# First block sums of a two-level Strassen output: a unit later by DMA in three units of four, on VectorE in the fourth

## The chip, the cores and the metric

One NeuronCore of a Trainium2 chip runs the whole program. The metric is the device time of one execution in microseconds (us). Engine names: PE is TensorE, PEld its weight loads, DVE VectorE, ACT ScalarE, POOL GpSimd, SP SyncE; the q after a name (SPq, POOLq) marks the engine's own queue.

## The reference

The program computes a channel attention and then a SiLU feed-forward network on its output:

```python
qn = q / (norm(q, axis=1) + 1e-6);  kn = k / (norm(k, axis=1) + 1e-6)   # q, k, v: (2, 6016, 256)
s = kn.transpose(0, 2, 1) @ qn / tau                                    # (2, 256, 256)
a = softmax(s)
x = (v @ a).reshape(12032, 256)
h = x @ w_in                                                            # w_in: (256, 2048)
out = (h / (1 + exp(-h))) @ w_out                                       # w_out: (2048, 256)
```

All in float32. On the chip, every operand of a large product is kept as two float16 parts (high and low), and a product is three float16 matmuls.

## The kernel before

The 12032 tokens are cut into 12 "pairs" `p` of two token blocks, 1024 tokens wide (896 in pairs 5 and 11). Pairs 0 and 5 run an older path (`emit_pair_group`, L682, 8 groups each; "the old pairs"), the other ten the path with units (`emit_unit`, L729, 8 units `u` each, 80 in all; `paired` holds these pairs). In the paired pairs the order of PE, DVE and ACT is the order in which the code writes the instructions; POOL and SP are ordered by a scheduler.

A unit works on one half of the pair's tokens (`t = u // 4`) and a quarter of the hidden width (`q = u % 4`), in four slots, one after each `yield`. Its seven input products go into three PSUM banks `y`, `x`, `z`, allocated once at L48. Slot 0 writes y, x and z; slot 1 adds to y and x; slot 2 and slot 3 add to x. ACT copies y and x out (L780, L782, L790), DVE takes differences (L760), ACT applies SiLU (L763) and makes the high parts of the hidden blocks (L770), DVE the low parts (L773). Four blocks come out of a unit: b11, b12 (the "tops") and b21, b22 (the "lows").

`out_of_unit` (L852 to L971) is the output side. Per unit it queues eleven "items" of four matmuls each on average (`add`, line L866 of the trace) into the list `ready`. They accumulate in four PSUM banks per half, a, b, c and d, from a pool of four (`ps_o`). Some items read the blocks, four read sums of blocks: t1 = b11 + b12, t3 = b12 + b22, t2 = t3 + b11, t4 = t2 + b21. The sums t2 and t3 are two DVE instructions in slot 2 of the next unit (`plus`, L940). The sum t1 is made by POOL's DMA queue in `first_sum`: a copy of b11 into a buffer (L946), then, when it has landed, an accumulating copy of b12 on top (L949). The sum t4 is made in the same way a unit later (copy of t2, L948; accumulating copy of b21, L951), except in the last unit of a half (`own`), where DVE makes it. In the trace L946 and L949 are t1's two DMAs, L948 and L951 are t4's, and the matmuls of t1 read `sums` with the weights `ws_lo`/`ws_hi`, those of t4 read `sums` with `wo`.

The code of unit u's output side runs as a list of steps by slot (`later`): in unit u+1, slot 0 the low part of the tops, `first_sum` and the high part of the lows; in slot 1 the low part of the lows; in slot 2 `other_sums`, which appends the unit's items to `ready`. After each slot the main loop runs items from `ready`: 2, 3, 4 and 2 of them in slots 0 to 3 (`room_left` 8, 12, 16, 8 at cost 4). So the eleven items of unit u run from slot 2 of unit u+1 to slot 1 of unit u+2, and the last of them reads t1. t4's item of unit u is put just ahead of t1's item of unit u+1 (`behind_one`).

After the last unit of a half (q = 3) the four banks are copied out by ACT (`take`, L910): c, a, b, d in slots 0, 1, 2, 3 of unit u+2. In slot 3 DVE also combines them (`join`, four L925 instructions, and `leave(0)`, one L929 and a store); `leave(1)` (L929, store) is in slot 0 of unit u+3.

In the same slots DVE and ACT prepare the next pair's operand (`scale_v`, 15 steps). They are taken in units 2, 3, 4, 6 and 7, in three slots each: slots 1 to 3 up to pair 3, slots 0 to 2 from pair 4 on. The load of the next v (`load_v`, L485, 1 MB on SP) starts when the buffer of the last one is free.

Of the kernel before, what the change touches and what calls it, by code (L numbers as in the profile page):

```python
# [8 lines left out]
F16 = mybir.dt.float16  # L9
# [9 lines left out]
P = 128  # L19
# [11 lines left out]
def channel_attention_then_silu_ffn(ctx, tc, kq, qT, kT, vT, tau, w_in, w_out, outT):  # L31
# [13 lines left out]
    hp = ctx.enter_context(tc.tile_pool(name="hp", bufs=1))  # L45
    sm = ctx.enter_context(tc.tile_pool(name="sm", bufs=2))
    ps_b = ctx.enter_context(tc.tile_pool(name="ps_b", bufs=1, space=PSUM))
    z, y, x = (ps_b.tile([P, 512], F32, tag=k, name=k) for k in "zyx")  # L48
    ps_o = ctx.enter_context(tc.tile_pool(name="ps_o", bufs=4, space=PSUM))

    ident = const.tile([P, P], F32, name="ident")
# [13 lines left out]
    rtau = const.tile([P, 1], F32, name="rtau")  # L65
    tiny = const.tile([P, 1], F32, name="tiny")
    nc.vector.memset(tiny, 1e-30)
    junk = const.tile([1, 1], F32, name="junk")
    ws_hi = const.tile([P, 4, NI, P], F16, name="ws_hi")

# [20 lines left out]
    def small_psum(name):  # L91

        if early[0]:
            return ps_o.tile([P, 512], F32, tag="o", name=name)
        return z

    @contextmanager
    def at(priority):
# [583 lines left out]
    def emit_pair_group(p, i):  # L682
# [7 lines left out]
        def product(bank, a, x, first=False):  # L690
            for j, (u, y) in enumerate(((1, 0), (0, 1), (0, 0))):
                nc.tensor.matmul(
                    bank[:, :h], wm[:, u, a - 1], m[:, y, x, :h], start=(first and j == 0),
                    stop=(j == 2), skip_group_check=True,
                )

        def copy(bank, t):
            nc.scalar.copy(t[:, :h], bank[:, :h])
            return t
# [8 lines left out]
        def silu(src, g, row, l):  # L708
            nc.scalar.activation(out=g[:, :h], in_=src[:, :h], func=AF.Silu, scale=alpha)
            return {"p": p, "f": 2 * i + (row == 1), "l": l, "h": h, "g": g, "sg": sg}  # L710

        product(y, S1, T1, True)
        c51 = hp.tile([P, 2, 512], F32, tag="c51", name="c51")
        c5 = copy(y, c51[:, 0])
        product(x, A11, B11, True)
        c1 = copy(x, c51[:, 1])
        product(z, A12, B21, True)
        g11 = minus(c1, z)
        tail(0)
# [20 lines left out]
    def emit_unit(p, u):  # L740
# [2 lines left out]
        b, n, w = pairs[p]  # L743
        h = w // 2
        m, alpha, sg = parts[p]
        which = 2 * (u % 4), 2 * (u % 4) + 1
        wide = h // 2
        at = u // 4 * wide
# [80 lines left out]
    def out_of_unit(p, u, blocks, rest_top, high_low, rest_low):  # L829
# [10 lines left out]
        if "14" not in sums:  # L840
            sums["14"] = vp.tile([P, 2, 2, 2, 512], F16, tag="v", name="sums", bufs=3)
        t23 = st.tile([P, 2, 2, 512], F16, tag="st", name="t23", bufs=7)
        w1, w4 = (sums["14"][:, u % 2, k] for k in range(2))
        t1, t4, t2, t3 = (k[:, :, :h] for k in (w1, w4, t23[:, 0], t23[:, 1]))

        def bank(name):
# [28 lines left out]
        def cross(kind, e, x):  # L875
            return [(kind, e, x, 1, 0), (kind, e, x, 0, 1)]

        def high(e, x1, x2):
# [8 lines left out]
            add("d", 0, high(1, b11, b21), False),  # L887
            add("d", 1, high(1, b12, b22), end),
        ]
        fourth = add("d", 0, cross(0, 1, t4), end)  # L890
        then = [
            add("a", 1, cross(-2, 1, t2), end),
            add("b", 0, cross(-3, 1, t3), end),
            *behind_one,
            add("b", 1, cross(-1, 1, t1), end),
        ]
        behind_one[:] = []
        if own:
            then.append(fourth)
        else:  # L900
            behind_one.append(fourth)
        s = {}

        def take(name):
# [34 lines left out]
        def plus(o, x, y):  # L939
            nc.vector.tensor_tensor(out=o, in0=x, in1=y, op=ALU.add)  # L940

        def first_sum():
            if last:
                plus(t1, b11, b12)
                return
            nc.gpsimd.dma_start(w1, blocks[0])  # L946
            for o, x, y in fourths:
                nc.gpsimd.dma_start(o, x)  # L948
            nc.gpsimd.dma_start(w1, blocks[1], accum_op=ALU.add)  # L949
            for o, x, y in fourths:  # L950
                nc.gpsimd.dma_start(o, y, accum_op=ALU.add)  # L951
            fourths[:] = []

        def other_sums():
            ready.extend(now)
            plus(t3, b12, b22)
            plus(t2, t3, b11)
            if own:
                plus(t4, t2, b21)
            else:  # L960
                fourths.append((t4, t2, b21))
            ready.extend(then)
# [2 lines left out]
        later(1, rest_low)  # L965
        later(2, other_sums)
        if end:
            for k, name in enumerate("cabd"):
                later(4 + k, lambda name=name: take(name), order=1)
            later(7, join, lambda: leave(0), order=2)  # L970
            later(8, lambda: leave(1), order=2)  # L971

    def prepare_sums():

# [274 lines left out]
    fixed = ExitStack()  # L1249
    for p, (b, n, w) in enumerate(pairs):  # L1250
        fixed.close()
        if p in paired:
            fixed.enter_context(
                tc.manual_schedule(
                    engines={
                        mybir.EngineType.PE, mybir.EngineType.DVE, mybir.EngineType.Activation
                    }
                )
            )
# [5 lines left out]
        for i in range(NI):  # L1265
# [30 lines left out]
            for _ in (emit_unit if p in paired else emit_pair_group)(p, i):  # L1296
# [3 lines left out]
                if p == 0 and i < 2:  # L1300
                    prepare()
                take = 2 if p == 0 and i > 2 and len(pending) > 4 - slot else 1
                room_left = (8, 12, 16, 8)[slot] if p in paired else 12 * take
                queue = ready if p in paired else pending
                while queue and room_left > 0:
                    cost, run = queue.pop(0)
# [3 lines left out]
                if p == 0 and i < NI - 1:  # L1310
                    nextmix = background(nextmix)
                if p in paired:
                    if i in (2, 3, 4, 6, 7) and slot in ((1, 2, 3) if p < 4 else (0, 1, 2)):
                        vgen = background(vgen)
                elif i >= 1 and vgen is not None and (
                    p == 0 or slot in ((0, 2) if not last else (0, 2, 3) if i > 4 else (2, 3))
                ):
                    vgen = background(vgen, 2 if p == 0 else 1)
# [62 lines left out]
```

## Time and profile before

| what | us |
|---|---|
| median of 3 runs (lowest to highest) | 1063.17 (1061.96 to 1067.81) |
| the profiled execution, its own time | 1060.87 |
| its span in the trace | 1059.1 |
| PE busy | 1015.2 (96%) |
| DVE busy | 831.7 (79%) |
| ACT busy | 800.8 (76%) |
| POOL busy | 207.7 (20%) |
| mean granted TensorE clock | 0.989 |

The span is what the trace shows from the first to the last event; the execution's own time is 1.8 us more. A busy share is a mean over the whole span; PE's includes time at either clock level.

### The profile page before, as it was taken

How to read it: one execution, taken by the hardware profiler on the slowest of the kernel's cores; microseconds unless marked ns; L12 is line 12 of the kernel's file. 1: busy time of each engine (PE TensorE's matmuls, PEld its weight loads, DVE VectorE, ACT ScalarE, POOL GpSimd, SP SyncE). 2: the span in 40 equal slices, each digit the busy share in tenths (PEclk: the TensorE clock that was granted, in tenths of full speed). 3: DMA queues.
4: the chain of work that ended last, by engine and by line, in shares of the span. 5: the costliest groups of instructions: out<-in, count | busy, mean ns of one | idle time of the engine just before them, and what ended most of it. 6: DMA issues, size and time to landing. Idle time of an engine off the chain costs nothing. (4 is left out here: it accounts for less than half of the span.)

```text
span 1059.1 us, 20486 instructions
## 1 busy us (share of the span) xinstructions
PE 1015.2 (96%) x8222; PEld 841.5 (79%) x8222; DVE 831.7 (79%) x1339; ACT 800.8 (76%) x1161; POOL 207.7 (20%) x299
## 2 busy tenths in 40 slices
PE   9999999998999799999999999999999999999985
PEld 8876555787888688878655688888888888889985
DVE  6998577778779588978789788888788878888764
ACT  6687687887778579778778778778678787787763
POOL 0010000122221222222100022222222222222231
PEclk9999999999999899999999999999999999999998
DMA  9996010557546465544301244545545445444442
GB/s 369 395 400 207 1 40 1 173 134 219 162 120 165 138 189 138 142 103 100 101 20 32 65 114 111 146 109 135 135 97 155 118 98 148 120 104 120 112 113 65
DMA packets 62544, 143.34 MB, mean 135 GB/s; under 512 B 6898, under 2 KB 19010, under 8 KB 62450
## 3 DMA queue, kind: packets, MB, share of 16 engines
q0 software_dynamic: 31696, 72.57, 29.4%
q1 hardware_dynamic: 30466, 68.95, 18.5%
q8 instruction: 64, 1.05, 0.4%
q10 hardware_dynamic: 288, 0.52, 0.1%
q14 instruction: 30, 0.25, 0.1%
HBM read 57.67 MB, written 12.32 MB: 66 GB/s over the span
## 5 line engine op out<-in xcount | busy, mean ns | idle before, releaser
L753 PEld LDWEIGHTS <-wall 128*128 128x128 f16 x3360 | 328.4, 98 | 49.4 <-issue 12.9
L753 PE MATMUL x<-m,wall 128*128 128x256 f16 (+1 forms) x1920 | 260.7, 272 | 8.4 <-ACT c L790 3.5
L773 DVE SCALAR_TENSOR_TENSOR hl<-g,sg,hl 128x1024 f16<-128x1024 f32 (+1 forms) x160 | 203.0, 1269 | 76.1 <-ACT hl L770 74.8
L866 PE MATMUL o<-hl,wo 128*128 128x256 f16 (+1 forms) x1920 | 248.7, 273 | 0.5 <-DVE hl L773 0.5
L866 PEld LDWEIGHTS <-wo 128*128 128x128 f16 x2240 | 220.3, 99 | 27.9 <-issue 2.9
L763 ACT ACTIVATE g<-g,alpha 128x1024 f32<-128x1024 f32 (+3 forms) x160 | 146.0, 927 | 88.7 <-DVE g L760 86.5
L770 ACT ACTIVATE hl<-g,sg 128x1024 f16<-128x1024 f32 (+1 forms) x160 | 181.5, 1135 | 0.0
L753 PE MATMUL y<-m,wall 128*128 128x256 f16 (+1 forms) x960 | 129.8, 271 | 0.1
L949 POOL DMA_DIRECT2D sums<-hl x79 | 67.2, 851 | 278.7 <-DMA sums<-hl 206.6
L946 POOL DMA_DIRECT2D sums<-hl x79 | 57.9, 733 | 227.7 <-DMA outT<-sb 103.8
L951 POOL DMA_DIRECT2D sums<-hl x59 | 51.8, 878 | 184.9 <-DMA sums<-t 48.4
L760 DVE TENSOR_TENSOR g<-x,c 128x512 f32<-128x512 f32 (+1 forms) x80 | 54.5, 681 | 42.6 <-PE x L753 42.5
L661 PE MATMUL o<-hl,wo 128*128 128x512 f16 (+1 forms) x384 | 87.2, 366 | 0.1
L790 ACT COPY c<-x 128x512 f32<-128x512 f32 (+1 forms) x80 | 46.5, 581 | 54.0 <-PE x L753 53.8
L866 PEld LDWEIGHTS <-ws_hi 128*128 128x128 f16 x640 | 62.9, 98 | 29.8 <-issue 23.0
L763 ACT ACTIVATE g<-x,alpha 128x512 f32<-128x512 f32 (+1 forms) x80 | 54.3, 679 | 29.9 <-PE x L753 27.7
L866 PE MATMUL o<-t,ws_lo 128*128 128x256 f16 (+1 forms) x320 | 76.7, 271 | 0.0
L866 PE MATMUL o<-t,ws_hi 128*128 128x256 f16 (+1 forms) x320 | 76.7, 271 | 0.0
L760 DVE TENSOR_TENSOR g<-c,y 128x512 f32<-128x512 f32 (+1 forms) x80 | 54.3, 679 | 28.3 <-ACT c L790 27.8
L300 PE MATMUL sc<-kq_t 128*128 128x256 f32 x320 | 74.6, 385 | 0.5 <-DMA kq_t<-in_kq 0.4
L300 PEld LDWEIGHTS sc<-kq_t 128*128 128x128 f32 x320 | 61.0, 193 | 11.6 <-DMA kq_t<-in_kq 1.7
L661 PEld LDWEIGHTS <-wo 128*128 128x128 f16 x384 | 37.6, 98 | 39.1 <-issue 0.9
(194 smaller groups left out, 1608.0 us busy)
## 6 DMA issues: line engine op xcount, KB each, us to landing
sums<-hl POOLq DMA_DIRECT2D x212, 256.0 KB, 3.3
kq_t<-in_kq SPq DMA_DIRECT2D x39, 512.0 KB, 8.8
sums<-t POOLq DMA_DIRECT2D x54, 256.0 KB, 2.8
v_t<-in_vT SPq DMA_DIRECT2D x10, 1024.0 KB, 6.2
outT<-sb SPq DMA_DIRECT2D x40, 256.0 KB, 2.5
turned<-in_qT SPq DMA_DIRECT2D x10, 512.0 KB, 4.8
turned<-in_kT SPq DMA_DIRECT2D x10, 512.0 KB, 5.7
raw<-in_w_in SPq DMA_DIRECT2D x5, 512.0 KB, 10.5
```

Source lines behind the costliest of these rows:

```text
L300: nc.tensor.matmul(sc[:, cb, :], t[:, i, 0, cb * P : (cb + 1) * P], t[:, i, 1, :], start=(j + i == 0 and cb == 0), stop=(j + i == J - 1), ...
L661: nc.tensor.matmul(o[:, :h], a[:, f, ee], hl[:, m, :h], start=(c == 1 and i == 0), stop=(c == NF and i == 2),)
L753: nc.tensor.matmul(bank[:, k * wide : (k + 1) * wide], mixed[b, i][:, v, a - 1], m[:, c, x, at : at + wide], start=(first and j + k == 0), ...
L760: nc.vector.tensor_tensor(out=g, in0=a[:, :h], in1=c[:, :h], op=ALU.subtract)
L763: nc.scalar.activation(out=g, in_=src, func=AF.Silu, scale=alpha)
L770: nc.scalar.activation(out=hl[:, :, 0], in_=g, func=AF.Copy, scale=sg)
L773: nc.vector.scalar_tensor_tensor(out=hl[:, :, 1], in0=g, scalar=sg, in1=hl[:, :, 0], op0=ALU.mult, op1=ALU.subtract,)
L790: nc.scalar.copy(c2[:, :h], x[:, :h])
L866: nc.tensor.matmul(o[:, side * wide : (side + 1) * wide], a, x, start=(first and j == 0), stop=(last and j == len(these) - 1), skip_group_ ...
L946: nc.gpsimd.dma_start(w1, blocks[0])
L949: nc.gpsimd.dma_start(w1, blocks[1], accum_op=ALU.add)
L951: nc.gpsimd.dma_start(o, y, accum_op=ALU.add)
```

## The change

- t1 of a unit that is not `own` is still made by DMA, but its item (with t4's item) moves to the end of the next unit's list: `others` in `behind_one`. It needs one more buffer, `extra`.
- In an `own` unit (the fourth of each half; in the last half also the third) DVE makes t1, as one more `plus` in `other_sums`, into a tile of its own with t4 (`t14`, from the pool of `st` buffers). `first_sum` then issues only t4's DMAs of the unit before.
- The copies out of the banks: c, a as before, b one slot later (slot 3 of unit u+2), d one slot later (slot 0 of unit u+3), `leave(0)` in slot 0 and `leave(1)` in slot 1 of unit u+3.
- The 15 steps of `scale_v` are spread 3, 4, 1, 3, 4 over units 2, 3, 4, 6, 7 instead of 3 each.
- In the last unit of the program 3 items instead of 4 run in slot 2, and none in slot 3 (`over`); the rest follows after it.
- y, x and z are allocated per group in the old pairs, and once per run of paired pairs in the others (`firsts`).

```diff
-    z, y, x = (ps_b.tile([P, 512], F32, tag=k, name=k) for k in "zyx")
+    firsts = {}
+    extra = const.tile([P, 2, 512], F16, name="extra")
-        return z
+        return firsts["z"] if firsts else ps_b.tile([P, 512], F32, tag="z", name=name)
 # emit_pair_group
+        y = ps_b.tile([P, 512], F32, tag="y", name="y")
+        x = ps_b.tile([P, 512], F32, tag="x", name="x")
...
+        z = ps_b.tile([P, 512], F32, tag="z", name="z")
 # emit_unit
+        if not firsts:
+            firsts.update({k: ps_b.tile([P, 512], F32, tag=k, name=k) for k in "zyx"})
+        x, y, z = (firsts[k] for k in "xyz")
 # out_of_unit
-        w1, w4 = (sums["14"][:, u % 2, k] for k in range(2))
+        w1, w4 = (*(sums["14"][:, k, 0] for k in range(2)), extra)[q % 3], sums["14"][:, q % 2, 1]
+        if own:
+            t14 = st.tile([P, 2, 2, 512], F16, tag="st", name="t14", bufs=7)
+            w1, w4 = (t14[:, k] for k in range(2))
-        fourth = add("d", 0, cross(0, 1, t4), end)
+        others = [add("b", 1, cross(-1, 1, t1), end), add("d", 0, cross(0, 1, t4), end)]
             *behind_one,
-            add("b", 1, cross(-1, 1, t1), end),
+            *(others if own else ()),
         ]
-        behind_one[:] = []
-        if own:
-            then.append(fourth)
-        else:
-            behind_one.append(fourth)
+        behind_one[:] = [] if own else others
         def first_sum():
-            if last:
-                plus(t1, b11, b12)
-                return
-            nc.gpsimd.dma_start(w1, blocks[0])
-            for o, x, y in fourths:
+            these = [*([] if own else [(w1, *blocks[:2])]), *fourths]
+            for o, x, y in these:
                 nc.gpsimd.dma_start(o, x)
-            nc.gpsimd.dma_start(w1, blocks[1], accum_op=ALU.add)
-            for o, x, y in fourths:
+            for o, x, y in these:
                 nc.gpsimd.dma_start(o, y, accum_op=ALU.add)
 # other_sums
             if own:
+                plus(t1, b11, b12)
                 plus(t4, t2, b21)
         if end:
-            for k, name in enumerate("cabd"):
-                later(4 + k, lambda name=name: take(name), order=1)
-            later(7, join, lambda: leave(0), order=2)
-            later(8, lambda: leave(1), order=2)
+            for k, name in (4, "c"), (5, "a"), (7, "b"), (8, "d"):
+                later(k, lambda name=name: take(name), order=1)
+            later(7, join, order=2)
+            later(8, lambda: leave(0), order=2)
+            later(9, lambda: leave(1), order=2)
 # main loop
+        if p not in paired:
+            firsts.clear()
-                room_left = (8, 12, 16, 8)[slot] if p in paired else 12 * take
+                over = p == len(pairs) - 1 and i == NI - 1
+                room_left = (8, 12, 16 - 4 * over, 8 - 8 * over)[slot] if p in paired else 12 * take
-                    if i in (2, 3, 4, 6, 7) and slot in ((1, 2, 3) if p < 4 else (0, 1, 2)):
+                    many = {2: 3, 3: 4, 4: 1, 6: 3, 7: 4}.get(i, 0)
+                    if slot in ((), (3,), (), (1, 2, 3) if p < 4 else (0, 1, 2), range(4))[many]:
                         vgen = background(vgen)
```

## Rows read from the trace of the kernel before

**Rows 1.** The page: busy time, share and instructions of each engine.
```profile
PE 1015.2 (96%) x8222; PEld 841.5 (79%) x8222; DVE 831.7 (79%) x1339; ACT 800.8 (76%) x1161; POOL 207.7 (20%) x299
```
**Rows 2.** PE's longest wait over the span: us in total, times, longest.
```profile
PE o L866 <- DMA sums<-hl: 22.9, 10, 4.4
```
**Rows 3.** PE's groups by shape: count, busy, mean ns, idle before them and what ended it.
```profile
L866 PE MATMUL o<-sums,ws_lo 128*128 128x256 f16 x144 | 35.9, 276 | 13.1 <-DMA sums<-hl 12.9
...
L866 PE MATMUL o<-sums,ws_lo 128*128 128x224 f16 x16 | 3.9, 272 | 8.0 <-DMA sums<-hl 8.0
```
**Rows 4.** Stretches at half clock: length, then busy PE, PEld, DVE, ACT, POOL, PEclk, DMA.
```profile
263.98:267.38 3.40, 2.92 (x14) 2.02 (x14) 0.60 (x1) 0.00 (x0) 0.97 (x2) 0.50 0.20 82
345.90:356.13 10.23, 5.85 (x29) 4.19 (x28) 2.67 (x4) 0.72 (x1) 3.05 (x5) 0.50 0.59 162
1045.63:1049.03 3.40, 2.70 (x15) 2.20 (x15) 0.56 (x1) 0.00 (x0) 0.00 (x0) 0.50 0.05 8
```
**Rows 5.** Timeline at one wait: start, length, engine, line; in brackets the idle time before.
```profile
253.81 0.38 SPq L485 DMA_DIRECT2D v_t<-in_vT  x1
254.28 1.86 SPq L256 DMA_DIRECT2D turned<-in_qT  x3
...
256.10 0.85 POOL L949 DMA_DIRECT2D sums<-hl  x1 [3.29 <-DMA sums<-hl]
...
264.45 0.37 PE L866 MATMUL o<-sums,ws_lo 128*128 128x256 f16 x1 [3.35 <-DMA sums<-hl]
```
**Rows 6.** Timeline of POOL and PE in an undisturbed unit.
```profile
860.93 0.86 POOL L946 DMA_DIRECT2D sums<-hl  x1
...
866.57 0.85 POOL L949 DMA_DIRECT2D sums<-hl  x1 [4.78 <-DMA sums<-hl]
...
870.27 0.60 PE L866 MATMUL o<-sums,wo 128*128 128x256 f16 x4
...
870.70 0.27 PE L866 MATMUL o<-sums,ws_lo 128*128 128x256 f16 x1
```
**Rows 7.** DMAs into `sums`: us from issue to landing, least, median, most.
```profile
DMA to landing us min/median/max: 2.3/3.3/9.5
```
**Rows 8.** Timeline at the one wait of t4's item.
```profile
345.31 0.60 PE L866 MATMUL o<-sums,wo 128*128 128x256 f16 x4 [1.92 <-DMA sums<-hl]
```
**Rows 9.** Timeline of PE and ACT in slot 0 of a unit with a copy out.
```profile
867.65 0.60 PE L866 MATMUL o<-hl,wo 128*128 128x256 f16 x4
868.73 0.68 ACT L910 ACTIVATE sb<-o,back 128x512 f32<-128x512 f32 x1
```
**Rows 10.** Timeline of DVE and PE in unit 2 of a pair from pair 6 on.
```profile
838.15 1.28 DVE L773 SCALAR_TENSOR_TENSOR hl<-g,sg,hl 128x1024 f16<-128x1024 f32 x1
...
839.35 0.68 DVE L929 TENSOR_TENSOR sb<-sb 128x512 f32<-128x512 f32 x1
...
839.95 0.68 DVE L760 TENSOR_TENSOR g<-c,z 128x512 f32<-128x512 f32 x1
...
845.32 0.82 PE L753 MATMUL x<-m,wall 128*128 128x256 f16 x6 [0.38 <-DVE g L760]
```
**Rows 11.** Timeline of DVE and PE in unit 6 of a pair from pair 6 on.
```profile
882.36 0.68 DVE L760 TENSOR_TENSOR g<-x,c 128x512 f32<-128x512 f32 x1
...
883.09 0.81 PE L753 MATMUL x<-m,wall 128*128 128x256 f16 x6
```
**Rows 12.** DVE's block sums by shape, and DVE's wait for the lows' and tops' high parts.
```profile
L940 DVE TENSOR_TENSOR t<-hl 128x1024 f16<-128x1024 f16 x72 | 49.1, 682 | 0.0
...
DVE hl L773 <- ACT hl L770: 74.8, 82, 3.2
```
**Rows 13.** PE's wait in slot 2 after a copy out and a square on ACT (pair 1).
```profile
233.14 0.81 PE L753 MATMUL x<-m,wall 128*128 128x256 f16 x6 [0.19 <-ACT c L790]
```
**Rows 14.** Timeline of the end: DVE's last low part and PE's last wait for a sum.
```profile
1043.01 1.15 DVE L773 SCALAR_TENSOR_TENSOR hl<-g,sg,hl 128x896 f16<-128x896 f32 x1
...
1046.33 0.35 PE L866 MATMUL o<-sums,ws_lo 128*128 128x224 f16 x1 [4.38 <-DMA sums<-hl]
```

## The prediction

> **What bounds the kernel now.** I read the page first: PE is busy in 96% of the span, DVE and POOL far less [rows 1], so time can only be won where PE stands still or runs slowly, and it is lost where another engine makes PE wait. The view of PE's waits then names one cause that is larger than all others together: the output products wait for DMAs into `sums`, 22.9 us in 10 waits [rows 2]. The groups by shape say which product that is: t1's items, with 12.9 us in the wide pairs and 8.0 us in the narrow last one [rows 3]; what is left, 1.9 us, is a single wait of t4's item [rows 8].
>
> The timeline shows why. In an undisturbed unit t1's copy is issued at 860.93 and the accumulating copy at 866.57, because POOL waits for the landing in between; with the median landing of 3.3 us [rows 7] the sum is there at 869.9, and its item starts at 870.70 [rows 6]: 0.8 us to spare. Where a load of v and three more loads are issued just ahead (253.81 and 254.28), the accumulating copy of 256.10 is late: the item starts at 264.45, 8.35 us after its issue, having waited 3.35 us [rows 5]. So t1 is nearly late in every unit, and any load on the DMA queues turns that into a wait of PE.
>
> Three of these waits also cost clock. In the stretches at half clock (0.50 is the lower of the two levels, 1.2 GHz) PE worked for 2.92, 5.85 and 2.70 us [rows 4]. Each begins while PE stands still for a sum. Half of that work, 11.47 / 2 = 5.7 us, would be saved at full clock. The waits and the clock together are 28.6 us.
>
> The Trainium skill ("TensorE: Matmul & The Clock Gate", Terms) puts the penalty at the time below full rate times the share of pulses lost; that is 17.03 x 0.5 = 8.5 us by the lengths of the same stretches. The rows decide here: in 5.6 us of these stretches PE had nothing to do, and that time is already in the waits.
>
> **t1 a unit later (three units of four).** Nothing changes in the work of PE: the same four matmuls run, ten items on average further down. A unit is 9.4 us long (x in slot 3 of two units that lie four apart starts at 845.32 and 883.09, [rows 10, 11]; the difference over 4). t1's room grows from 0.8 to about 10 us, and the longest landing in the whole trace, 9.5 us against a median of 3.3 [rows 7], is only 6.2 us over. I take all of t1's waits, 20.9 us, as gone in these units.
>
> **t1 on DVE (one unit of four).** Twenty more sums of 0.68 us [rows 12], 13.6 us of DVE, one in each unit after an `own` unit; the one of the last unit was there already, and the third unit of the last half adds one more. They stand in slot 2 behind PE's needs of that slot. DVE afterwards waits for ACT's high part in most units, 74.8 us in 82 waits, 0.9 us each [rows 12], which is more than 0.68. Units 4 and 0 have the added sum; unit 4 gives up two preparation steps and unit 0 has none. I take 0. If that cover were gone it would cost 20 x 0.68 = 13.6 us at most. POOL loses 40 DMAs, and so 40 x 256 KB of traffic; I count nothing for it.
>
> **t4 stays where it was.** Its DMAs are issued in the same slot as before and its item moves back by one item, 0.43 us (four matmuls; 870.70 - 870.27 in [rows 6]). The one wait of 1.92 us [rows 8] then leaves 1.5 us. Beside it, the fourth sum of the next unit queues on POOL behind the late t1 and may be late once or twice: I take 2.0 us in all, bounds 0 and 8 (four such waits of 2).
>
> **The copies out.** c and a keep their slots. b goes into slot 3, d into slot 0 of the next unit, behind the high part of the lows. On ACT this moves 0.68 us into slot 0. Behind it there stand the copy of c2 (L790), for which PE's x product of slot 2 waits, and in pairs 1 to 3 a square of 1.05 us. The same sequence stands in the trace already, one unit earlier, with the copy of c: there PE's x product waited 0.19 us [rows 13]. Six such halves (pairs 1 to 3) give 1.1 us; bounds 0 and 4 (six times 0.7).
>
> On DVE `leave(0)` comes into slot 0 where `leave(1)` was, and `leave(1)` into slot 1, ahead of the two differences on which x in slot 3 waits. In unit 2 from pair 4 on, where two maxima of v are in the way, PE already waits 0.38 us for DVE there. One more L929 takes 0.60 us of a busy DVE (839.35 to 839.95); `leave(0)` used to stand ahead of 838.15 and gave 0.15 of that [rows 10], so PE's wait grows by 0.45. In unit 6 the difference ends at 883.04 and x starts at 883.09 [rows 11]: no cover is left, so 0.45 to 0.5 us there as well. Six pairs (4, 6 to 10) times two halves times 0.47 are 5.7 us. In pairs 1 to 3 slot 0 has no preparation step in these units, which leaves some 0.7 us or more of cover: nothing. Bounds: 0 and 12 (1 us in each of the 12).
>
> **The rest.** In the last unit x of slot 3 runs one item earlier (0.4 us), and PE has those items left while ACT and DVE finish the last blocks. Its wait of 4.38 us for t1 goes. What is late next is DVE's last low part, which ends at 1044.16 [rows 14], some 0.4 us earlier after the change; the items that PE still has reach to about 1043. I take 0.5 us of wait, bounds 0 and 1.5. In the old pairs PE is without gaps before, so new tiles of x, y and z can win nothing there; a worse order may cost up to 3 us, and I take 0. A PE that is not held up meets ACT and DVE less rested: 1 us, bounds 0 and 3, for the short waits that the stalls now hide.
>
> **The sum.** -28.6 + 2.0 + 1.1 + 5.7 + 0.5 + 1.0 = -18.3 us against the profiled execution's own 1060.87 us (span 1059.1 and 1.8 around it): 1042.6. The median of the runs is 2.3 us above that execution; such a spread is what late DMAs make, and most of them go, so I forecast 1043. With all costs at their low ends (0) it is 1060.87 - 28.6 = 1032; with t4, DVE and ACT at their high ends (8, 12 and 4) and 2 for the rest it is 1058.
>
> **Rivals.** (1) The wait moves from t1 to t4. POOL takes its DMAs in a scheduled order, and up to now t4's go ahead of t1's. If t1's went first, t4 would inherit the 0.8 us to spare. Each of nine waits would then be shorter only by the item's 0.43 us, about 4 us in all, with one of three clock losses gone, 2 us; with the costs above the time would be 1060.9 - 6 + 7 = 1062, no change. Against it: t4's inputs are ready a slot or more ahead of t1's, and in the trace its item waits once in the whole span. The Trainium skill ("DMA: Bandwidth & Descriptors", Anatomy of one DMA) puts a GpSimd DMA at 2.0 us plus its bytes over 436 GB/s, by my estimate 2.6 us for 256 KB. By that no sum would ever be late and this rival, like the gain, would be nothing; the 8.35 us of [rows 5] says otherwise, so the rows decide.
>
> (2) Slower: PE waits for the copy out of d. The next half's first product into its bank d is the second item of slot 0 of unit u+3, the very slot into which d's copy moves. PE reaches the second item 0.43 us after 867.65, at 868.08; a copy out in that place starts at 868.73 and ends at 869.41 [rows 9]: 1.3 us of wait. This happens in 18 changes of half: 18 x 1.3 = 24 us, and with the sum above 1067. It decides if the new d is given the bank of the old d. The pool hands out the bank that came free first, and that is b's, copied out a slot earlier; new b then takes d's. The order of copies out and of first products speaks for this, no row shows the bank.
>
> (3) DVE becomes the bound in units 6 and 7, and 2 and 3. It has four steps in units 3 and 7 now, behind units 2 and 6 with two `leave`s. If each of 20 halves costs 0.8 us instead of 12 costing 0.47, that is 16 us instead of 5.7: 1053.
>
> (4) The change does not do what it says: the loads that made t1 late make something else late (the loads wait for `st` buffers, of which `t14` takes one), and the time stays near 1060.
>
> **Chances.** The forecast 0.66 (1035 to 1050 by its own range), rival 1 0.07, rival 2 0.10, rival 3 0.12, rival 4 0.05. What a measurement of this kernel can tell from no change is about 0.5%, 5.3 us, so faster means under 1057.9 and slower over 1068.5. The forecast and rival 3 are faster, with a little of rival 4: 0.79. Rival 1, most of 4 and a part of 2 (at 1067 it lies near the edge) are no change: 0.14. Slower, the larger part of 2: 0.07. The range from 1034 to 1056 takes in the forecast and rival 3 and leaves out 0.2.
>
> **What would show it.** PE's waits should have no `sums` above 3 us in all; no stretch at half clock should begin behind a sum. L949's count falls from 79 to 59, DVE's block sums rise by 21, and PE's waits on DVE's differences (L760) and on ACT's copies (L790) rise by 6 and 1 us. Rival 1 shows as waits of the items with `wo`; rival 2 as PE waits on L910; rival 3 as waits on L760 in every pair. I am wrong if PE's busy time does not fall by the 5.7 us of clock, or if a new wait of more than 5 us stands in PE's list.

## The result and the profile after

| what | before | after |
|---|---|---|
| median of the runs (lowest to highest), us | 1063.56 (1061.96 to 1067.81) | 1034.37 (1033.76 to 1036.43) |
| ratio, 95% interval | | 0.9723, 0.9691 to 0.9755 |
| the profiled execution, its own time, us | 1060.87 | 1034.91 |
| its span, us | 1059.1 | 1033.1 |
| mean granted TensorE clock | 0.989 | 0.999 |

The change is faster by 2.8%. The forecast was 1043 with a range from 1034 to 1056. The direction was right and the time lies at the lowest edge of the range; two of the four runs, 1033.76 and 1033.82, lie below it. The profiled execution fell by 26.0 us where the sum had 18.3.

Lines move by a few: the differences of L760 are now L767, the output items of L866 are L876, ACT's copy of c2 (L790) is L797, the copies out (L910) are L916, `leave` (L929) is L935, the copies of the sums (L946, L948) are L951 and the accumulating ones (L949, L951) are L953, DVE's `plus` is L946.

The page's first line (to be read beside [rows 1]) and PE's longest waits (beside [rows 2]; us in total, times, longest):

```profile
PE 1006.9 (97%) x8222; PEld 837.5 (81%) x8222; DVE 844.1 (82%) x1359; ACT 799.2 (77%) x1161; POOL 180.0 (17%) x259
```
```profile
PE x L760 <- DVE g L767: 8.0, 12, 1.2
PE x L760 <- ACT c L797: 4.0, 10, 1.6
PE x L693 <- ACT c L699: 2.3, 2, 2.0
...
PE o L876 <- DMA sums<-hl: 0.9, 1, 0.9
PE x L760 <- ACT g L770: 0.8, 1, 0.8
```

PE does the same 8222 matmuls in 8.3 us less busy time, of which 7.4 are clock (half of PE's busy time in the stretches at half clock: 5.7 of [rows 4], and 1.7 of a stretch told of below). The 22.9 us of waits for sums have become 0.9. What leads the list now is new: DVE's differences, 8.0 us where the list of before had 2.6. PE's groups by shape (beside [rows 3]) show that no item of t1 waits any more; the one wait left is t4's, in the narrow last pair:

```profile
L876 PE MATMUL o<-sums,ws_lo 128*128 128x256 f16 x72 | 17.7, 273 | 0.0
L876 PE MATMUL o<-extra,ws_lo 128*128 128x256 f16 x36 | 8.8, 273 | 0.0
...
L876 PE MATMUL o<-sums,wo 128*128 128x224 f16 x20 | 2.7, 259 | 0.9 <-DMA sums<-hl 0.9
```

The same two places as the first two in [rows 4], unit 0 of pairs 2 and 3, by stretch (length, busy PE, PEld, DVE, ACT, POOL, then PEclk): PE has no gap and the full clock in both.

```profile
255.00:265.00 10.00, 10.00 (x94) 8.96 (x93) 7.83 (x13) 8.14 (x13) 0.84 (x1) 1.00 0.84 271
331.00:341.00 10.00, 10.00 (x94) 8.95 (x93) 7.83 (x13) 8.14 (x13) 0.84 (x1) 1.00 0.87 275
```

The landings themselves are no better than in [rows 7] (first those into `sums`, then those into the new buffer `extra`, which holds the t1 of the third unit of a half), and POOL still stands behind them. The timeline at the load of v of [rows 5] shows it: POOL waits 8.26 us for one landing, and the item of t1, whose accumulating copy was issued at 252.39, starts at 267.93 without a wait, 15.5 us later.

```profile
DMA to landing us min/median/max: 2.3/3.3/8.3
```
```profile
DMA to landing us min/median/max: 2.3/3.5/9.2
```
```profile
251.85 0.38 SPq L486 DMA_DIRECT2D v_t<-in_vT  x1
252.32 6.49 SPq L257 DMA_DIRECT2D turned<-in_qT  x3
252.39 0.84 POOL L953 DMA_DIRECT2D extra<-hl  x1 [2.96 <-DVE g L767]
...
263.09 0.84 POOL L953 DMA_DIRECT2D sums<-hl  x1 [8.26 <-DMA sums<-t]
...
267.93 0.27 PE L876 MATMUL o<-extra,ws_lo 128*128 128x256 f16 x1
```

Where did the time go? I cut both traces at the first z product of each unit. Up to the first unit 1.56 us were won, from the first unit's z to the last unit's z 19.84, behind it 4.58: 25.98 in all. By the unit's number in its pair (summed over the ten pairs; minus is a gain), beside the same table for experiments told of below:

| us from z to z, unit | 0 | 1 | 2 | 3 | 4 | 5 | 6 | 7 |
|---|---|---|---|---|---|---|---|---|
| before to after | -16.4 | -0.2 | +2.3 | -0.3 | -6.9 | -2.1 | +2.8 | +1.0 |
| after to leaves late (e3) | 0.0 | 0.0 | -5.0 | 0.0 | 0.0 | 0.0 | -4.3 | +0.2 |
| after to fourth by DMA (e4) | 0.0 | +5.7 | 0.0 | 0.0 | 0.0 | +1.9 | +0.1 | 0.0 |
| leaves late to fixed banks, leaves late (e12) | 0.0 | 0.0 | +10.8 | 0.0 | 0.0 | 0.0 | +13.9 | -0.2 |

The gain sits in units 0 and 4, where the t1 of the third unit of a half (q = 2) came due, and in the narrow pair's unit 5; the loss sits in units 2 and 6, where the two `leave`s are. In the wide pairs a load was issued beside the chain of the late sum each time. In the narrow last pair, with 8.0 of the 20.9 us [rows 3], none did: in the kernel before, POOL's own queue (q0) is the only one that moved bytes from 1000 to 1012 us, and the item waited 1.86 us all the same. There a unit is only 8.24 us long, so the item comes due sooner behind a chain of ordinary landings. An undisturbed unit of a wide pair takes 9.39 us in both kernels.

```profile
q0 software_dynamic: 577, 0.98, 38.0%
```
```profile
1009.75 0.26 PE L866 MATMUL o<-sums,ws_lo 128*128 128x224 f16 x1 [1.86 <-DMA sums<-hl]
```

### The profile page after: what moved, and what is told of

The parts are those of the page before. It is cut to its first block, busy times and chain, and to the rows that moved or that the text cites. A ratio compares the mean times of both kernels' runs of the same rounds, so it can differ in the third digit from the quotient of the medians.

```text
span 1033.1 us, 20363 instructions
## 1 busy us (share of the span) xinstructions
PE 1006.9 (97%) x8222; PEld 837.5 (81%) x8222; DVE 844.1 (82%) x1359; ACT 799.2 (77%) x1161; POOL 180.0 (17%) x259
## 4 chain that ended last, share of the span: by engine, by line
PE 68%; DVE 13%; ACT 12%; DMA 4%; issue 3%; POOL 0%; DVEq 0%; SPq 0%; ACTq 0%; POOLq 0%
PE o L876 26%; PE x L760 16%; PE y L760 7%; PE o L662 6%; PE sc L301 4%; PE z L760 4%; ACT hl L777 3%; DVE hl L780 2%; DVE g L767 2%; PE x L693 2%; DVE sb L935 1%; PE w L441 1%; DVE av L148 1%; PE y L693 1%; ACT g L770 1%
## 5 line engine op out<-in xcount | busy, mean ns | idle before, releaser
L760 PEld LDWEIGHTS <-wall 128*128 128x128 f16 x3360 | 327.6, 98 | 54.3 <-issue 18.9
L760 PE MATMUL x<-m,wall 128*128 128x256 f16 (+1 forms) x1920 | 259.2, 271 | 13.2 <-DVE g L767 8.0
L876 PE MATMUL o<-hl,wo 128*128 128x256 f16 (+1 forms) x1920 | 249.2, 271 | 0.2 <-DVE hl L780 0.2
L876 PEld LDWEIGHTS <-wo 128*128 128x128 f16 x2240 | 218.8, 98 | 24.7 <-issue 1.5
L953 POOL DMA_DIRECT2D sums<-hl x99 | 85.9, 867 | 291.0 <-DMA sums<-hl 103.9
L760 PE MATMUL y<-m,wall 128*128 128x256 f16 (+1 forms) x960 | 129.7, 271 | 0.1
L876 PE MATMUL o<-t,ws_lo 128*128 128x256 f16 (+1 forms) x362 | 86.8, 271 | 0.0
L876 PE MATMUL o<-t,ws_hi 128*128 128x256 f16 (+1 forms) x362 | 86.8, 271 | 0.0
L951 POOL DMA_DIRECT2D sums<-hl x40 | 29.4, 735 | 303.0 <-DVE hl L780 123.7
L797 ACT COPY c<-x 128x512 f32<-128x512 f32 (+1 forms) x80 | 46.5, 581 | 38.8 <-PE x L760 38.2
L767 DVE TENSOR_TENSOR g<-x,c 128x512 f32<-128x512 f32 (+1 forms) x80 | 54.4, 680 | 23.8 <-PE x L760 23.7
L767 DVE TENSOR_TENSOR g<-c,y 128x512 f32<-128x512 f32 (+1 forms) x80 | 54.2, 678 | 23.1 <-ACT c L797 22.8
L946 DVE TENSOR_TENSOR t<-t,hl 128x1024 f16<-128x1024 f16 (+1 forms) x101 | 69.0, 683 | 2.7
L876 PEld LDWEIGHTS <-ws_hi 128*128 128x128 f16 x640 | 62.6, 98 | 6.8
```

The costliest lines, as they stand in the source:

```text
L760: nc.tensor.matmul(bank[:, k * wide : (k + 1) * wide], mixed[b, i][:, v, a - 1], m[:, c, x, at : at + wide], start=(first and j + k == 0), ...
L767: nc.vector.tensor_tensor(out=g, in0=a[:, :h], in1=c[:, :h], op=ALU.subtract)
L797: nc.scalar.copy(c2[:, :h], x[:, :h])
L876: nc.tensor.matmul(o[:, side * wide : (side + 1) * wide], a, x, start=(first and j == 0), stop=(last and j == len(these) - 1), skip_group_ ...
```

## The experiments

**The sums alone (e1).** From the kernel before, only the change to `first_sum`, `others`, `extra` and `t14`. Against the changed kernel it reads:

```diff
-            for k, name in (4, "c"), (5, "a"), (7, "b"), (8, "d"):
-                later(k, lambda name=name: take(name), order=1)
-            later(7, join, order=2)
-            later(8, lambda: leave(0), order=2)
-            later(9, lambda: leave(1), order=2)
+            for k, name in enumerate("cabd"):
+                later(4 + k, lambda name=name: take(name), order=1)
+            later(7, join, lambda: leave(0), order=2)
+            later(8, lambda: leave(1), order=2)
...
-                    many = {2: 3, 3: 4, 4: 1, 6: 3, 7: 4}.get(i, 0)
-                    if slot in ((), (3,), (), (1, 2, 3) if p < 4 else (0, 1, 2), range(4))[many]:
+                    if i in (2, 3, 4, 6, 7) and slot in ((1, 2, 3) if p < 4 else (0, 1, 2)):
```

(and x, y, z and the last unit's items as before).

> The kernel before with the change to the sums alone (t1 a unit later by DMA in three units of four, on DVE in the fourth); copies out, preparation steps, tiles of x, y, z and the last unit as before. My theory (the gain is t1's wait and its clock, and each other part has its own small price): the waits for sums fall from 22.9 to under 3 us here, no stretch at half clock begins behind one; the 5 us of DVE waits in units 2 and 6 that the moved leave steps add are absent, and PE ends a little later in the tail (about 1 us). That gives 1029 to 1033. Rival (the copies further apart are needed, since the sums on DVE need the room): PE's waits on DVE's differences and on ACT's copies rise here by more than 8 us, and the time is 1040 or more.

Measured: 1039.82 us (1038.06 to 1041.80), ratio 0.9761 (0.9729 to 0.9792). The gain is there, but neither of my numbers was right: the time lies between the two theories, and I had expected the DVE waits of units 2 and 6 to be gone, and they are as large as in the whole change.

```profile
PE x L754 <- DVE g L761: 8.0, 12, 1.5
PE x L754 <- ACT c L791: 4.2, 8, 1.6
...
PE x L754 <- ACT g L764: 2.0, 1, 2.0
...
PE o L870 <- DMA sums<-hl: 1.0, 1, 1.0
```

The timeline of unit 1 of pair 8 shows why (ACT's copy out of b, then DVE's `join` and `leave(0)`):

```profile
741.42 0.69 ACT L910 ACTIVATE sb<-o,back 128x512 f32<-128x512 f32 x1 [1.23 <-PE o L870]
...
742.91 1.87 DVE L925 TENSOR_TENSOR sb<-sb 128x256 f32<-128x256 f32 x4
...
744.70 0.69 DVE L929 TENSOR_TENSOR sb<-sb 128x512 f32<-128x512 f32 x1
```

With t1's item deferred, the half's list is one item longer in its last unit, and bank b is complete one item later. In its old slot 2 ACT waits 1.23 us for that bank, with the SiLU behind it, and `take` pulls items forward until the bank is complete, which puts a fifth item into slot 2. Everything behind it, the two `leave`s too, comes late. So the later copies out are not a separate piece of the change; they follow from the deferral.

**The changed kernel again (e8), and with the old spread of the preparation steps (e7).** The edit of e7 is the last part of the diff above alone.

> The changed kernel itself once more, as the base for the other runs of this call. Every theory: 1033 to 1037, and the same waits unit by unit (8.0 us for DVE's difference, about 4 for ACT's copy, under 1.5 for sums).

> The changed kernel with the preparation steps spread as before (3 each in units 2, 3, 4, 6 and 7). The sums alone cost 4 to 5 us more than the whole change, and this says which other part gives that. Theory (the later copies out: with the sums moved, bank b is complete one item later, and the old place of its copy pulls an item forward and makes ACT wait 1.2 us): within 1.5 us of the changed kernel here. Rival (the spread gives it, since unit 4 has one step in place of three beside the added sum on DVE): 3 to 5 us above the changed kernel, with PE waits in unit 4.

Measured: e8 1034.77 us (1034.17 to 1036.54); e7 1036.11 us (1035.06 to 1036.64). The spread is worth 1.3 us by the medians, though the runs of the two overlap. By units, e7 is 1.0 us longer, and that is mostly one place: unit 4 of pair 4 (+1.12; +1.12 and +1.13 in e1 and e11, which have the old spread too), where PE's wait of 2.0 us for ACT stands again:

```profile
PE x L760 <- ACT g L770: 2.0, 1, 2.0
```

So what e1 lacks of the whole change, about 5 us, is by subtraction mostly the place of the copies out; no run here has the whole change without that part alone. Units 2 and 6 don't change with the spread (0.0 and -0.3 us).

**The fourth unit's t1 by DMA again (e4).**

```diff
-            these = [*([] if own else [(w1, *blocks[:2])]), *fourths]
+            these = [*([] if over and own else [(w1, *blocks[:2])]), *fourths]
...
-                plus(t1, b11, b12)
+                if over:
+                    plus(t1, b11, b12)
```

(`over` is here the last half of the program.)

> The changed kernel, but t1 of the own unit is made by DMA again as before (in the last half on DVE as in the changed kernel). My theory (being a unit later is what frees t1; the fourth on VectorE matters little, since of the ten waits before only one, 1.95 us in the narrow last pair, was that of an own unit): within 1.5 us of the changed kernel, with 0 to 3 us of waits for sums and DVE 13 us less busy. Rival (40 DMAs fewer on POOL are what frees the queue, for t4's chain too): 5 to 10 us of waits for sums come back and the time rises by as much.

Measured: 1042.88 us (1041.30 to 1046.24), ratio 0.9792 (0.9763 to 0.9822), 8 us above the changed kernel. My theory fell. The rival was right in its numbers, but not in the part on t4's chain: what waits is the own unit's t1 itself (`t`, 5.6 us), and t4's wait stays at 0.6 us.

```profile
PE o L876 <- DMA t<-hl: 5.6, 3, 3.2
```
```profile
263.69 0.84 POOL L953 DMA_DIRECT2D sums<-hl  x1 [8.95 <-ACT g L770]
264.43 0.67 POOL L951 DMA_DIRECT2D t<-hl  x1
...
268.06 0.84 POOL L953 DMA_DIRECT2D t<-hl  x1 [2.96 <-DMA t<-hl]
...
272.69 0.37 PE L876 MATMUL o<-t,ws_lo 128*128 128x256 f16 x1 [3.17 <-DMA t<-hl]
```

POOL reaches t1's copy of the own unit only at 264.43, behind an accumulating copy that stood 8.95 us (this view names ACT; at the same place in the changed kernel it names the landing of a copy, 8.26 us); the sum is 3.17 us late, a stretch of 3.4 us at half clock begins in that wait, and the unit loses 4.6 us. The kernel before showed no such wait here, and I had read that as room. It was shelter: PE had already stood 3.35 us for the t1 of the unit ahead [rows 5] and had then worked at half clock, and that gave the own unit's t1 its time. The trace of before bears it out:

```profile
270.77 0.86 POOL L949 DMA_DIRECT2D sums<-hl  x1 [2.96 <-DMA sums<-hl]
...
275.25 0.27 PE L866 MATMUL o<-sums,ws_lo 128*128 128x256 f16 x1
```

The accumulating copy of 270.77 was down 3.3 us later by the median landing, 1.2 us ahead of its item, and the unit ahead had lost 4.9 us. Without that loss the sum would have been some 3.7 us late (an estimate from these rows); e4 has 3.2. With the first stall gone, the second one appears. By units 5.4 of e4's loss stand in unit 1 of pairs 2 and 3, right behind the two units that had lost most in the kernel before (4.9 and 9.5 us); the 1.9 in unit 5 are the narrow pair's own wait, which the kernel before had too.

**POOL in the written order (e6),** from the kernel before:

```diff
-                        mybir.EngineType.PE, mybir.EngineType.DVE, mybir.EngineType.Activation
+                        mybir.EngineType.PE, mybir.EngineType.DVE, mybir.EngineType.Activation,
+                        mybir.EngineType.Pool,
```

> The kernel before with POOL in the written order as well: copy of b11, copy of t2, then the two accumulating copies, so that t1 has no landing of t4 ahead of it and waits for one landing in place of two or three. Theory A (t1 was late because t4's chain stood ahead of it on POOL): waits for sums fall from 22.9 to under 10 us, and the time to 1045 to 1052. Theory B (the loads of v and of the other operands stretch each landing, whatever the order): over 15 us of waits for sums stay, and the time is within 6 us of the kernel before.

Measured: 1045.88 us (1044.61 to 1047.03), ratio 0.9851 (0.9816 to 0.9886). The waits are between the two theories, 11.6 us, and the time is in A's range: the order alone was worth some 15.7 us against the kernel before beside it (1061.62). The rows tell more than the sum: every wait for a sum is now t4's, and none t1's. The summary of PE's waits, and the longest one in the timeline:

```profile
PE o L866 <- DMA sums<-hl: 11.6, 7, 3.9
```
```profile
342.92 1.01 PE L866 MATMUL o<-sums,wo 128*128 128x256 f16 x4 [3.90 <-DMA sums<-hl]
343.73 0.42 PE L866 MATMUL o<-sums,ws_lo 128*128 128x256 f16 x1
```

So t1 was late because t4's chain stood ahead of it on POOL, and t4 is late once t1's stands ahead of it. This is the mechanism of the prediction's first rival. In the changed kernel t4 still goes first, and it is t1 that has a unit of room. POOL issues four DMAs per unit, and each of the two accumulating copies has to wait until the copy under it has landed; neither of the two orders brought both sums in time.

**The copies out and the spread without the sums (e2, e9, e10),** from the kernel before: both (e2), the spread alone (e9), the copies out and leaves alone (e10). The edits are the two parts of e1's diff, the other way round.

> The kernel before with only the moved copies out, the moved leave steps and the new spread of the preparation steps; the sums as before. My theory: PE's waits on DVE's differences rise by some 5 us (12 units of a pair from pair 4 on, 0.45 to 0.5 each) and those on ACT's copies by about 1, the waits for sums stay at about 20 us: 1066 to 1070 against a median before near 1063.5. Rival (the spread takes DVE and ACT out of the way where the loads come, and so helps the sums): waits for sums under 15 us and a time of 1060 or less.

> The kernel before with only the new spread of the preparation steps (3, 4, 1, 3, 4); sums and copies out as before. The copies and the spread together came out at 1060.6 in place of the 1066 to 1070 that I expected, although their DVE waits were there (8.0 against 2.6 us). Theory A (the spread moves the steps that free v's buffer, so the loads and the sums collide differently, at 5 us or so less): 1055 to 1060 here, with fewer or shorter waits for sums than 22.9 us. Theory B (the spread does nothing to the sums, as it did nothing in the changed kernel, 1.3 us): within 3 us of the kernel before.

> The kernel before with only the copies out and the leave steps moved; sums and spread as before. Price by rows: 5.4 us more of PE's waits on DVE's differences. Theory A (the spread is what made the two together cheap): 1066 to 1070. Theory B (the waits in units 2 and 6 give the sums of the next units time, so that part of the price comes back): 1060 to 1065, with waits for sums at 20 us or less.

| kernel | median, us (lowest to highest) | ratio to before, run beside it |
|---|---|---|
| e2, both | 1060.61 (1056.67 to 1065.31) | 0.9943 (0.9917 to 0.9969) |
| e9, spread | 1061.69 (1057.42 to 1066.36) | 0.9969 (0.9944 to 0.9994) |
| e10, copies out and leaves | 1068.78 (1065.22 to 1075.14) | 1.0040 (1.0013 to 1.0067) |

PE's waits of e2, then those of e10:

```profile
PE o L866 <- DMA sums<-hl: 23.1, 16, 4.5
PE x L753 <- DVE g L760: 8.0, 12, 1.2
```
```profile
PE o L866 <- DMA sums<-hl: 22.2, 12, 4.7
PE x L753 <- DVE g L760: 7.7, 12, 1.2
```

The price of the leaves' new place is there in both, as forecast: 5.1 to 5.4 us more than the 2.6 of before, in 12 waits where before had 6. In e10 it shows in the time (+0.4%, about 4 us), as its theory A had it; e9 lies between its two theories. In e2 it does not: the time went the other way, and the spread's own gain (0.3%) is too small to explain it. The three traces show 22 to 25 us of waits for sums, but each is one execution (e2's is the slowest of its ten), and these kernels' runs lie 9 to 10 us apart. The ten runs of e2 had a granted clock of 0.991 to 0.996, the runs of before beside them 0.984 to 0.991, so e2 lost less to half clock; which of the waits got shorter is not settled by these runs.

**The leaves behind the difference (e3),** from the changed kernel:

```diff
-            later(8, lambda: leave(0), order=2)
-            later(9, lambda: leave(1), order=2)
+            later(10, lambda: leave(0), order=2)
+            later(11, lambda: leave(1), order=2)
```

> The changed kernel with the two leave steps of a half in slots 2 and 3 of unit u+3 instead of slots 0 and 1, so that both stand behind the difference on which x in slot 3 waits. My theory (the 6 us added in units 2 and 6 are these two DVE instructions ahead of that difference): PE's waits on DVE's difference fall from 8.0 to about 2 us and the time by 5 to 7 us, to 1028 to 1030. Rival (it is DVE's total work in these units that PE waits for, wherever the steps stand): the time stays within 2 us of the changed kernel, and the wait moves to the low part or to unit 3.

Measured: 1025.25 us (1025.06 to 1026.36), ratio 0.9625 (0.9602 to 0.9648), 9.1 us below the changed kernel and the fastest of all. The timeline of DVE and PE in unit 2 of pair 8, the changed kernel first: both leaves stand ahead of the last difference, which x in slot 3 waits for. In e3 they stand behind it, and x doesn't wait.

```profile
742.94 0.68 DVE L935 TENSOR_TENSOR sb<-sb 128x512 f32<-128x512 f32 x1
...
746.46 0.68 DVE L935 TENSOR_TENSOR sb<-sb 128x512 f32<-128x512 f32 x1
...
748.79 0.68 DVE L767 TENSOR_TENSOR g<-x,c 128x512 f32<-128x512 f32 x1
...
749.52 0.82 PE L760 MATMUL x<-m,wall 128*128 128x256 f16 x6 [0.85 <-DVE g L767]
```
```profile
744.55 0.68 DVE L767 TENSOR_TENSOR g<-x,c 128x512 f32<-128x512 f32 x1
...
745.47 0.82 PE L760 MATMUL x<-m,wall 128*128 128x256 f16 x6
...
746.47 0.68 DVE L935 TENSOR_TENSOR sb<-sb 128x512 f32<-128x512 f32 x1
...
747.14 0.68 DVE L935 TENSOR_TENSOR sb<-sb 128x512 f32<-128x512 f32 x1
```
```profile
PE x L760 <- DVE g L767: 0.3, 1, 0.3
```

The wait of 8.0 us falls to 0.3, also the part that the kernel before had. The gain is larger than I expected, first because I had counted 0.38 us of before's own wait in unit 2 as DVE's load; it too was `leave`'s place. The waits account for 7.7 us of the 9.1. For the rest, a unit shrinks by some 0.15 us more than the wait that its row shows (unit 2 of pair 8 by 1.01 us, its wait was 0.85); why is open. DVE's total work is the same (844.8 us against 844.1), so place decides, not load.

**The same with the old spread (e11).** The edits of e3 and e7 together.

> The changed kernel with the leave steps in slots 2 and 3 of unit u+3 and the old spread of the preparation steps. The late leaves gave 9.1 us, the old spread cost 1.3. If the two don't meet: 1026 to 1028. If the new spread is needed only because the leaves stood in units 3 and 7's way: 1024 to 1025.5.

Measured: 1028.03 us (1026.00 to 1029.35), ratio 0.9660 (0.9633 to 0.9687): the two don't meet, and the new spread keeps its 1 to 3 us (1.1 by units of the two traces, 2.8 by the medians). Unit 4 of pair 4 is 1.13 us longer here too.

**Fixed banks (e5), and fixed banks with the leaves late (e12).** Each of a, c, d, b gets a bank of its own, so the new d takes the old d's bank:

```diff
-                banks[p, t, name] = ps_o.tile([P, 512], F32, tag="o", name="o")
+                banks[p, t, name] = ps_o.tile([P, 512], F32, tag="o" + name, name="o")
```

(the old pairs' outputs and the products ahead of the units are given the same tags, and the pool one buffer for each). In e12 `leave` stands as in e3.

> The changed kernel with each of the banks a, c, d and b in a place of its own, so that the new half's d is given the old d's bank and the new b the old b's. Theory of the second rival of the prediction (it is the rotation of the banks that keeps the late copy out of d free of charge): PE waits about 1.3 us for ACT's copy out of d in 18 changes of half, some 24 us, so 1055 to 1060, with the wait standing in PE's list as a first product of slot 0 behind the copy out. Rival (PE is never held up by the copy out): within 2 us of the changed kernel.

> The changed kernel with fixed banks and with the leave steps in slots 2 and 3 of unit u+3. Fixed banks alone put 21.9 us of waits for the copy out of d into PE's list, but took 7.7 us of its waits on DVE's differences out of it, and cost 14.4 us. Theory (the two waits shield each other: DVE catches up while PE stands at d): with the leaves late there is nothing left to shield, so the banks cost their full 20 to 22 us, and the time is 1046 to 1049, hardly below that with the leaves early. Rival (the two are separate, and the 14.4 us are the true price of the banks): 1025.3 + 14.4, so 1038 to 1041.

Measured: e5 1049.15 us (one execution); e12 1049.67 us (1049.56 to 1051.17), ratio 0.9864 (0.9826 to 0.9901). PE's waits, and one of the 18 in e5's timeline:

```profile
PE o L877 <- ACT sb L917: 21.9, 18, 1.5
...
PE x L761 <- DVE g L768: 0.3, 1, 0.3
```
```profile
752.81 0.68 ACT L917 ACTIVATE sb<-o,back 128x512 f32<-128x512 f32 x1
753.54 0.60 PE L877 MATMUL o<-hl,wo 128*128 128x256 f16 x4 [1.21 <-ACT sb L917]
```

The second rival's mechanism is real, and its waits were priced right: 18 of 1.2 us, 21.9 in all, where the prediction had 24. It didn't come because the pool gave the new d another bank. But in e5 it cost only 14.4 us, for while PE stands at d, DVE gets through its leaves and the 8.0 us of waits for it disappear. In e12, where DVE's waits are gone beforehand, the same 21.9 us of waits cost 24.4, and e5 and e12 are equal unit by unit (0.05 us from the first z to the last). In these units two waits were not a sum; the longer one hid the other.

## Why the prediction came out as it did

The bound and the mechanism were right. The waits for t1 go to zero, no half-clock stretch begins behind a sum (between 4 and 1031 us the trace has none at all), and t1's DMAs fall from 79 to 59, as POOL's groups by line show (40 accumulating copies into `sums` beside t4's 59, and 19 into `extra`):

```profile
L953 POOL DMA_DIRECT2D sums<-hl x99 | 85.9, 867 | 291.0 <-DMA sums<-hl 103.9 <-DMA sums<-t 80.9 <-ACT c L789 41.7
...
L953 POOL DMA_DIRECT2D extra<-hl x19 | 16.1, 848 | 45.9 <-DMA extra<-hl 26.2 <-DVE g L767 12.0 <-DVE t L946 7.8
```

Step by step:

- **t1 a unit later: right**, -20.9 us. The longest landing after, the 9.2 us into `extra` issued at 252.39, was still 6.3 us ahead of its item. The prediction's cause ("any load on the DMA queues") was too narrow, though: in the narrow pair t1 was late without one.
- **t1 on DVE at no cost: right in the number, wrong in what it was for.** DVE gets 20 more sums (182 to 202; I had counted 21) and PE waits for none of them. But I priced only its cost. That it also takes the own unit's t1 off POOL is worth 8 us (e4): of the gain of 26.0, the whole change without it leaves about 19 (the profiled execution of e4 has 1042.05 us).
- **Clock: 5.7 us as read**, and 1.7 more that I had left out of [rows 4]: a stretch at half clock ahead of the units. PE stands still near 84 to 86 us in both; the granted clock behind it differs by execution (before, then after):

```profile
84.00:92.00 8.00, 6.03 (x22) 4.12 (x21) 8.00 (x17) 8.00 (x14) 0.52 (x1) 0.79 0.63 207
```
```profile
84.00:92.00 8.00, 5.99 (x28) 4.42 (x27) 8.00 (x17) 8.00 (x14) 0.53 (x1) 1.00 0.78 254
```

  e8, the same kernel as after, has this stretch at half clock and is 1.5 us longer up to the first unit, so this part of the difference is not the change's.
- **t4: too dear.** Taken 2.0, measured 0.9, and that in the last pair (the line of PE's groups above). The one wait of before [rows 8] went entirely, not by the item's 0.43 us.

- **The leaves on DVE: right**, 5.7 forecast, 5.4 in PE's list, and by units +0.46 in unit 2 of pairs 4 and 7 to 10 and +0.48 to +0.52 in unit 6 of pairs 6 to 10, as [rows 10, 11] gave it; unit 6 of pair 4 grew by 0.18 only and unit 2 of pair 6 not at all. I took it as the price of the change; e3 shows that it was only the price of two slots.
- **The copies out on ACT: wrong place.** I expected +1.1 us in units 2 and 6 of pairs 1 to 3 by [rows 13]. None of these units got longer. Waits of 0.2 us came in unit 7 of these pairs, where the new spread has a fourth step, and one wait of 2.0 us for ACT's SiLU in pair 4 fell to 0.8 by the same spread (e7). Over all, ACT's waits of the x products fell by 0.7.
- **The tail and the rest: too dear.** 0.5 and 1.0 were taken; beside t4's wait above nothing shows. e1, which lacks the last unit's fewer items, ends behind its last unit's z within 0.03 us of the changed kernel, so that part did nothing measurable.

The 7.7 us between forecast and measurement are then 1.1 (t4), 1.7 (the early stretch), 1.8 (ACT), 0.3 (DVE), 1.5 (tail and rest), which is 6.4. Of the 1.3 us left, 0.9 stand in PE's busy time, which fell by 8.3 where the stretches at half clock give 7.4; why is open. All but the early stretch are costs that I sized above what the rows demanded. The range held because its low end was near the case in which the costs vanish, and it held by 0.4 us, less than the runs lie apart: that the median fell inside it is luck.

Rival 1 did not come, because POOL kept t4 ahead; e6 shows its mechanism in the kernel before as soon as the order is turned, but not its price: t4 inherited 11.6 of the 22.9 us, where I had let each wait shrink by 0.43 us only. Rival 2 did not come, and e5 shows its price. Rival 3 did not come: units 3 and 7 hold four steps and stay at their length, but for 0.5 us in unit 7 of pairs 1 and 2 and 0.4 us from unit 7 of pair 4 to the first unit of pair 6, which takes in the old pair 5. So the new tiles of x, y and z gained nothing there, as forecast.

## What to carry to other kernels

An item that waited for a chain of dependent DMAs was given room here by moving its use, while the landings stayed as late as they were and a new order of the DMAs only halved the waits (e6); after such a move look at what the old stall sheltered, because the next sum in the same queue became late when the first one no longer was (e4), and the same shelter made two waits in one unit cost less than their sum (e5, e12). When a step has to move on an in-order engine, put it behind the instruction that the bounding engine waits for next: two additions of 0.68 us, two slots further down, were worth 9 us (e3). And when an accumulation gets one item longer, move the copies out of its banks with it (e1).

## What the runs showed of the hardware

A 256 KB copy by POOL's queue, with a median landing of 3.3 us, took 8.3 us beside a load of v and three operand loads in the kernel before (issued at 256.10, the item that waits for it starts at 264.45 [rows 5]) and 9.2 in the changed one; the order of POOL's DMAs decided which sum bore it (e6), but with neither of the two orders did the waits go away. The Trainium skill ("DMA: Bandwidth & Descriptors", Anatomy of one DMA) gives 2.0 us plus the bytes over 436 GB/s, an estimate of 2.6 us here; the traces' least is 2.3, their median 3.3 to 3.4 and their longest 8.5 to 10.3, so the measurement decides: landings lie on both sides of the page's figure. Unexpected was also that the same wait of PE for ACT, 2.0 us long and over near 86.4 us, was followed by half clock in one execution and by full clock in another of the same program (e8 and the changed kernel).
